# Band rows of values loaded in two transfers per unit, and every store of x on SyncE's queue, in a local and global attention with a mixture of experts

## The chip, the cores and the metric

One core of a Trainium2 chip runs the whole program in one launch. The time is the device time of one execution in microseconds (us); the number for a kernel is the median over its runs. The engines are TensorE (PE in the rows, PEld for its weight loads), VectorE (DVE), ScalarE (ACT), GpSimd (POOL) and SyncE (SP). SP does no arithmetic: it issues transfers (DMAs). ACT and POOL can issue transfers too.

## The reference, cut to what matters

```python
batch, n_heads, seq, head_dim = (8, 8, 576, 64)            # q, k, v
q_d, k_d, v_d = means over 4 neighbouring positions        # 144 positions
out_up = repeat(softmax(q_d k_d^T / 8) v_d, 4)             # global part
mask = abs(pos[:, None] - pos[None, :]) < 4                # local part: a band of 7
out_local = softmax(where(mask, q k^T / 8, -1e9)) v
x = (out_up + out_local)                                   # 4608 tokens x 512
group = argmax(x w_group); expert = argmax(x w_expert[group])
out[token] = weight * relu(x w1[group, expert]) w2[group, expert]
```

There are 4 groups of 4 experts; each token goes to one of 16 experts, with a hidden size of 1024.

## The kernel before, in words

The attention works through 16 units. Unit u takes two batches and two heads (`Attention.unit`), 1152 query rows, and makes 128 of the 512 columns of x for the tokens of its two batches. Per unit the steps are: `load_k`, `load_q`, `load_v` (values pooled for the global part), `load_windows` (band rows of the values for the local part); `s_local`, `s_local_out`, `s_local_exp`, `soft_local` (band scores and their softmax in tile E); `s_down`, `s_down_max`, `s_down_exp`, `out_down`, `turn_down` (global part); `down_store` (L426, L427) writes the small global result to a scratch in DRAM and `load_down` (L431) reads it back into rows 96 to 127 of the tile `vw`; `turn_e` transposes E into `pt`; `x_bank` (L438) multiplies `pt` with `vw` and so makes x, local and global part in one product; `x_bank_out` copies it from PSUM to SBUF; `store_x` (L448) writes the unit's x, 576 KB, to DRAM; `turn_x`, `turn_x_out` and `logits` feed the router. `vw` holds, for 36 blocks of 32 queries, 48 rows of values for each of two heads (rows interleaved), so a row on its way is 64 numbers, 256 bytes.

`load_windows` (L205 to L223) issues four transfers for a unit, one for each head and batch (48 rows x 18 blocks), all from SyncE's queue. The values lie as (batch, head, position, feature). A block's band starts 8 rows ahead of its queries; at the ends of a batch these rows belong to a neighbour in memory, and the mask takes them out. Only the very first and the very last rows of the whole array have no neighbour, so the first and the last unit issue one transfer more (L221, L223). These are 66 transfers in all.

What sets the order of the work is a text, `ORDER`, written out ahead and run step by step (L1389) under a manual schedule: every engine and every queue does its share in exactly this order. A letter at the end of a step names the engine or the queue: A is ScalarE, D VectorE, P GpSimd, S SyncE. `store_x u A` therefore stands in ScalarE's own instruction stream; ScalarE issues the transfer and cannot go past it before it is issued. All loads stand in SyncE's stream. `fill n` is n matmuls that compute nothing that is used. Buffers: K, Q and pooled values have three each, `vw` three (two from unit 14 on), x three (`of`, L102), but from unit 14 on x has one, the one of units 0, 3, ..., 12. Weight tiles of the first expert (`raww`) lie where the attention's input tiles were.

The stretch around the change, in `ORDER` (lines of units 3 to 8):

```
turn_x 4 2; turn_pd_out 7 1 D; store_x 3 A; turn_x_out 4 2 A; load_q 10; turn_x_out 4 0 A; s_down 8; turn_pd_out 7 2 A; fill 12; x_bank 5 0
s_down_max 8; store_x 4 A; s_down_exp 8 0; out_down 7; down_store 6 S; s_down_exp 8 1; load_v 9; x_bank_out 5 2 A; s_local 9 0
```

The four PSUM banks of the pool `ps` are used in turn, so `x_bank 5 0` needs that `turn_x_out 4 0` has emptied one; the three of `psd` likewise, so `s_local 9 0` needs `s_down_exp 8 0`.

At the end of the attention the first expert starts: `early_expert` reads its number, `weights_in` (L826) loads its weights, `turn_in`, `hidden` (L875) and `project` (L921, L923) compute it. Then 14 more experts follow, each with its weights from DRAM, and the leftover rows of the first.

Of the kernel before, what the change touches and what calls it, by code (L numbers as in the profile page):

```python
# [31 lines left out]
NE = 16  # L32
NB = 4
# [20 lines left out]
class Attention:  # L54
# [9 lines left out]
    def __init__(self, tc, q, k, v, idf, xd, left, right, dram):  # L64
        nc = self.nc = tc.nc
        self.tc, self.q, self.k, self.idf = tc, q, k, idf
        n = NTOK * DM
        self.v, self.vm = v[0:n].rearrange("(b h s d) -> b h s d", h=H, s=S, d=D), v[n:].rearrange("(u p f) -> u p f", u=4 * NB, p=SD)
# [15 lines left out]
        one = cp.tile([1, 1], F32, name="one")  # L84
# [1169 lines left out]
turn_x_out 3 2 A; s_local 7 1; load_down 4 S; turn_x_out 3 1 A; turn_pd_out 6 1 D; turn_pd 6 0; logits 3; store_x 1 A; turn_pd 6 2  # L1254
load_v 7; turn_pd_out 6 0 A; s_local_out 7 1; s_local_exp 7 1; soft_local 6; turn_pd_out 6 2 D; x_bank 4 0; down_store 5 S
x_bank 4 2; x_bank_out 4 2 D; scores_out 0; load_windows 5; s_down 7; x_bank 4 1; scores_turn 0; x_bank_out 4 1 A; x_bank_out 4 0 D
scores_turn_out 0; out_down 6; turn_e 6 2; store_x 2 A; out_down_out 6 A; turn_e 6 0; s_down_max 7; turn_down 6; soft_down 6 P
# [9 lines left out]
turn_down_out 7; store_x 5 A; turn_x_out 5 1 A; soft_local 8; turn_x 5 0; load_q 11; x_bank 6 0; x_bank 6 2; s_down 9; pool_k 10 D  # L1267
turn_x_out 5 0 A; turn_pd 8 1; x_bank_out 6 0 A; turn_pd 8 2; x_bank_out 6 2 D; s_local_exp 9 0; s_down_max 9; s_local_exp 9 1
load_windows 7; turn_pd_out 8 1 A; pool_q 10 P; turn_pd_out 8 2 D; down_store 7 S; x_bank 6 1; s_down_exp 9 0; turn_e 8 1; load_k 11
# [3 lines left out]
s_local_out 10 0; soft_down 8 D; out_down_out 8 D; turn_x 6 2; turn_pd_out 9 2 A; s_local_exp 10 0; store_x 6 A; turn_down 8  # L1273
# [12 lines left out]
turn_pd 11 2; turn_e_out 10 1 A; turn_x 8 1; turn_e_out 10 2 A; turn_pd 11 0; turn_pd 11 1; store_x 7 A; turn_pd_out 11 2 A  # L1286
turn_x_out 8 1 A; s_local_out 12 1; soft_down 11 D; load_down 9 S; turn_pd_out 11 0 A; load_k 13; choose 1; store_x 8 A
# [5 lines left out]
turn_pd_out 12 0 A; turn_pd 12 2; soft_local_sum 12 D; store_x 9 A; turn_x 9 0; s_local 13 1; turn_x_out 9 1 A; turn_e_out 11 1 A  # L1293
# [8 lines left out]
turn_pd 13 2; s_local_out 14 1; turn_pd_out 13 0 A; turn_pd_out 13 2 A; store_x 10 A; turn_x 11 2; load_q 15; logits 10; turn_x 11 1  # L1302
# [3 lines left out]
store_x 11 A; s_local_out 15 1; turn_e_out 13 0 A; turn_e_out 13 2 A; s_local 15 0; lists_add 1; s_local_out 15 0; s_local_exp 14 0  # L1306
# [131 lines left out]
```

## Time and profile before

| | us |
|---|---|
| median of 3 runs | 750.79 |
| lowest and highest run | 750.01, 756.18 |
| the profiled execution, its time | 751.14 |
| its span, first to last instruction | 749.4 |

The profile is one execution. It has the busy time of each engine and each group of instructions, what an engine waited for ("<-" and the releaser), and for transfers their issue (a `q` after the engine's name, as SPq) and, where it is known, the time to landing. "PEclk" is the granted clock of TensorE in tenths of full speed (1.00 is 2.4 GHz, 0.50 is 1.2 GHz; numbers between are means over a stretch). The DMA share is the mean busy share of the core's 16 DMA engines. A matmul of fp32 operands stands as two records.

### The profile page before, as it was taken

The numbers are of one execution on the slowest core, as the hardware profiler recorded it, in microseconds if no ns is written. First come the engines' busy times: TensorE is split into PE (matmuls) and PEld (weight loads), VectorE is DVE, ScalarE is ACT, GpSimd is POOL, SyncE is SP. The second block draws the span as 40 slices with busy tenths as digits, with TensorE's granted clock in tenths as the row PEclk, the third lists the DMA queues.
The fourth block names the chain that finished last, engine by engine and source line by source line (L and its number), as shares of the span: only waits on it lengthen the run. The fifth ranks groups of instructions, "written<-read, shape, count | busy, mean of one in ns | idle before, by whom it ended". The sixth has DMA issues, their size and how long they took to land. (4 is left out here: it accounts for less than half of the span.)

```text
span 749.4 us, 20121 instructions
## 1 busy us (share of the span) xinstructions
PE 701.3 (94%) x8212; PEld 639.3 (85%) x8213; DVE 461.6 (62%) x834; ACT 362.7 (48%) x797; POOL 266.2 (36%) x307
## 2 busy tenths in 40 slices
PE   7789978999886979999999999999999999999996
PEld 4577766777665868998999999999999999999985
DVE  7877866999793765654545455464655555565541
ACT  4445535565573426543434444464554554555531
POOL 8975863585543650103111221302213213212211
PEclk9989999999998999999999999999999999999999
DMA  8879999898988463745455545646555665656600
GB/s 297 267 181 282 262 264 243 238 265 229 235 207 235 120 200 117 265 158 196 137 172 170 183 158 176 209 143 211 179 184 186 204 196 193 224 184 211 209 26 25
DMA packets 158243, 146.94 MB, mean 196 GB/s; under 512 B 69396, under 2 KB 129812, under 8 KB 158148
## 3 DMA queue, kind: packets, MB, share of 16 engines
q1 hardware_dynamic: 133540, 115.11, 51.7%
q0 software_dynamic: 7088, 21.66, 8.2%
q10 hardware_dynamic: 17520, 8.85, 4.5%
q8 instruction: 65, 1.06, 0.6%
q14 instruction: 30, 0.25, 0.1%
HBM read 124.29 MB, written 22.29 MB: 196 GB/s over the span
## 5 line engine op out<-in xcount | busy, mean ns | idle before, releaser
L846 POOL DMA_INDIRECT xg<-xd,gi x47 | 48.6, 1035 | 318.7 <-ACT yo L949 289.3
L875 PE MATMUL ph<-xh,w1h 128*128 128x256 f32 (+13 forms) x512 | 161.1, 316 | 0.0
L875 PE MATMUL ph<-xh,w1l 128*128 128x256 f32 (+13 forms) x512 | 156.1, 307 | 0.0
L875 PE MATMUL ph<-xl,w1h 128*128 128x256 f32 (+13 forms) x512 | 156.0, 306 | 0.0
L834 DVE TENSOR_TENSOR w2l<-raww,w2h 128x1024 fp32r<-128x1024 f32 x61 | 74.6, 1224 | 72.0 <-ACT w2h L833 56.5
L923 PE MATMUL y<-hl,w2h 128*128 128x416 f32 (+11 forms) x384 | 115.3, 311 | 0.0
L923 PE MATMUL y<-hh,w2l 128*128 128x416 f32 (+11 forms) x384 | 114.3, 308 | 0.0
L833 ACT ACTIVATE w2h<-raww 128x1024 fp32r<-128x1024 f32 x64 | 67.6, 1057 | 72.3 <-PE y L923 58.2
L875 PEld LDWEIGHTS ph<-xh,w1h 128*128 128x128 f32 x512 | 96.2, 188 | 1.5 <-issue 0.2
L834 DVE TENSOR_TENSOR w1l<-raww,w1h 128x1024 fp32r<-128x1024 f32 x60 | 73.4, 1224 | 38.8 <-ACT w1h L833 31.7
L875 PEld LDWEIGHTS ph<-xl,w1h 128*128 128x128 f32 x512 | 96.3, 188 | 0.9
L875 PEld LDWEIGHTS ph<-xh,w1l 128*128 128x128 f32 x512 | 96.1, 188 | 0.4
L880 DVE SCALAR_TENSOR_TENSOR hl<-ph,hh 128x256 fp32r<-128x256 f32 (+13 forms) x128 | 60.4, 476 | 55.3 <-ACT hh L879 50.6
L879 ACT ACTIVATE hh<-ph 128x256 fp32r<-128x256 f32 (+13 forms) x128 | 53.9, 422 | 75.7 <-PE ph L875 69.6
L923 PE MATMUL y<-hh,w2h 128*128 128x416 f32 (+11 forms) x384 | 87.7, 312 | 0.0
L833 ACT ACTIVATE w1h<-raww 128x1024 fp32r<-128x1024 f32 x64 | 67.5, 1057 | 32.0 <-PE ph L875 19.3
L950 POOL DMA_INDIRECT out_dram<-yo,oi x47 | 48.3, 1028 | 73.1 <-ACT yo L949 37.2
L923 PEld LDWEIGHTS y<-hh,w2l 128*128 128x128 f32 x384 | 72.3, 188 | 0.1
L923 PEld LDWEIGHTS y<-hl,w2h 128*128 128x128 f32 x384 | 72.2, 188 | 0.1
L923 PEld LDWEIGHTS y<-hh,w2h 128*128 128x128 f32 x384 | 62.9, 188 | 0.1
L438 PE MATMUL b_x<-vw,pt 128*32 128x128 f32 x1152 | 41.6, 287 | 6.9 <-DMA vw<-odd 4.3
L855 ACT ACTIVATE xh<-xt 128x256 fp32r<-128x256 f32 (+14 forms) x68 | 27.2, 420 | 34.3 <-PE xt L862 32.2
(225 smaller groups left out, 1287.1 us busy)
## 6 DMA issues: line engine op xcount, KB each, us to landing
raww<-in_moe_w_dram SPq DMA_DIRECT2D x128, 512.0 KB, 4.8
vw<-in_v_dram SPq DMA_DIRECT2D x62, 216.0 KB, 6.9
kt<-in_k_dram SPq DMA_DIRECT2D x16, 582.0 KB, 5.5
qT<-in_q_dram SPq DMA_DIRECT2D x16, 576.0 KB, 6.6
xd<-x ACTq DMA_DIRECT2D x15, 576.0 KB, 6.0
vs<-in_v_dram SPq DMA_DIRECT2D x16, 512.0 KB, 7.4
vw<-odd SPq DMA_DIRECT2D x16, 144.0 KB
odd<-odn SPq DMA_DIRECT2D x16, 128.0 KB
```

The lines of the kernel that those rows point to most:

```text
L438: self.nc.tensor.matmul(pt[32 * j : 32 * j + 32, t], self.of("pt", u)[:, 32 * lin : 32 * lin + 32], self.windows(u)[:, lin], start=True, s ...
L833: self.nc.scalar.activation(hi, raw, AF.Copy)
L834: eng.tensor_tensor(out=lo, in0=raw, in1=hi.bitcast(F32), op=ALU.subtract)
L846: self.nc.gpsimd.indirect_dma_start(out=xg[:w], out_offset=None, in_=self.xd[0:rows], in_offset=bass.IndirectOffsetOnAxis(ap=st["gi"][:w, ...
L855: self.nc.scalar.activation(hi, x, AF.Copy)
L875: nc.tensor.matmul(ph, a[:, k, cs], st[b][:, k], start=(n == 0), stop=(n == 11))
L879: nc.scalar.activation(hh, ph, AF.Relu)
L880: nc.vector.scalar_tensor_tensor(out=hl, in0=ph, scalar=0.0, in1=hh.bitcast(F32), op0=ALU.max, op1=ALU.subtract)
L923: nc.tensor.matmul(y, a[:, f % 2, cs], b, start=(f == 0 and n == 0), stop=(f == 7 and n == 2))
L950: i = nc.gpsimd.indirect_dma_start(out=self.out, out_offset=bass.IndirectOffsetOnAxis(ap=oi, axis=0), in_=yo[:m], in_offset=None, bounds_c ...
```

## The change

On the host the values are put as (pair of batches, head, batch, position, feature), with 8 rows of zeros ahead of the first and behind the last. The two batches of a pair then follow each other for each head, so the 36 blocks of a head have one stride, and `load_windows` issues two transfers of 48 rows x 36 blocks instead of four of 48 x 18; the transfers for the ends go. The rows and bytes are the same. In `ORDER` all `store_x` get the letter S. Most stay where they were; `store_x 5` goes behind `load_windows 7`, `store_x 12` behind `load_windows 14`, `store_x 13` behind `load_windows 15`, and `store_x 14` behind `weights_in 1`. `fill 12` goes. No other step moves.

```diff
-        n = NTOK * DM
-        self.v, self.vm = v[0:n].rearrange("(b h s d) -> b h s d", h=H, s=S, d=D), v[n:].rearrange("(u p f) -> u p f", u=4 * NB, p=SD)
+        n = NTOK * DM + 16 * D
+        self.v, self.vm = v[0:n], v[n:].rearrange("(u p f) -> u p f", u=4 * NB, p=SD)
...
-        s = self.st[u]
-        a = self.v[s["b0"], s["h0"], 0:1, :]
         for h in range(2):
-            dst = self.windows(u)[h : 2 * WW : 2, :, D * h : D * h + D]
-            for b in range(2):
-                o = a.offset + (b * H + h) * S * D
-                lo = 1 if o == 0 else 0
-                hi = NBLK - (o == (B * H - 1) * S * D)
-                dma = lambda rows, l, n: self.nc.sync.dma_start(
-                    out=dst[rows, NBLK * b + l : NBLK * b + l + n],
-                    in_=bass.AP(a.tensor, o + (32 * l - 8 + rows.start) * D, [[D, rows.stop - rows.start], [32 * D, n], [1, D]]),
-                )
-                dma(slice(0, WW), lo, hi - lo)
-                if lo:
-                    dma(slice(8, WW), 0, 1)
-                if hi < NBLK:
-                    dma(slice(0, 40), NBLK - 1, 1)
+            o = self.v.offset + (16 * (u // 4) + 4 * (u % 4) + 2 * h) * S * D
+            self.nc.sync.dma_start(
+                out=self.windows(u)[h : 2 * WW : 2, :, D * h : D * h + D],
+                in_=bass.AP(self.v.tensor, o, [[D, WW], [32 * D, 2 * NBLK], [1, D]]),
+            )
...
-turn_x 4 2; turn_pd_out 7 1 D; store_x 3 A; turn_x_out 4 2 A; load_q 10; turn_x_out 4 0 A; s_down 8; turn_pd_out 7 2 A; fill 12; x_bank 5 0
+turn_x 4 2; turn_pd_out 7 1 D; store_x 3 S; turn_x_out 4 2 A; load_q 10; turn_x_out 4 0 A; s_down 8; turn_pd_out 7 2 A; x_bank 5 0
...
-s_down_max 8; store_x 4 A; s_down_exp 8 0; out_down 7; down_store 6 S; s_down_exp 8 1; load_v 9; x_bank_out 5 2 A; s_local 9 0
+s_down_max 8; store_x 4 S; s_down_exp 8 0; out_down 7; down_store 6 S; s_down_exp 8 1; load_v 9; x_bank_out 5 2 A; s_local 9 0
...
-turn_e 15 0; store_x 14 A; turn_e_out 15 0 D; turn_x_out 14 0 D; turn_x 14 2; turn_x 14 1; turn_x_out 14 1 D; turn_x_out 14 2 A
+turn_e 15 0; turn_e_out 15 0 D; turn_x_out 14 0 D; turn_x 14 2; turn_x 14 1; turn_x_out 14 1 D; turn_x_out 14 2 A
...
-weights_split 0 w2 P; weights_in 1; turn_e 15 2; turn_e_out 15 2 D; x_bank 15 0; turn_in 2; x_bank_out 15 0 A; x_bank 15 1
+weights_split 0 w2 P; weights_in 1; store_x 14 S; turn_e 15 2; turn_e_out 15 2 D; x_bank 15 0; turn_in 2; x_bank_out 15 0 A; x_bank 15 1
...
-            a = _np.concatenate([a.reshape(-1), _np.concatenate([x.reshape(4 * NB, -1) for x in (two, one)], axis=1).reshape(-1)])
+            a = _np.pad(a.reshape(NB, 2, H, S, D).transpose(0, 2, 1, 3, 4).reshape(-1), (8 * D, 8 * D))
+            a = _np.concatenate([a, _np.concatenate([x.reshape(4 * NB, -1) for x in (two, one)], axis=1).reshape(-1)])
```

## Rows read from the trace of the kernel before

**Rows 1.** The page: the span in 40 equal slices of 18.7 us, tenths of TensorE's granted clock and of the DMA engines' busy share.

```profile
PEclk9989999999998999999999999999999999999999
DMA  8879999898988463745455545646555665656600
```

**Rows 2.** Busy time by stretch of the attention: start:end, length, then busy us (and instructions) of PE, PEld, DVE, ACT, POOL, the granted clock, the DMA share and GB/s.

```profile
58.00:110.00 52.00, 45.34 (x1122) 36.05 (x1121) 39.69 (x93) 26.01 (x89) 34.29 (x40) 0.98 0.99 278
110.00:126.00 16.00, 13.27 (x310) 10.81 (x313) 7.63 (x19) 7.51 (x23) 5.61 (x7) 0.84 0.94 215
126.00:176.00 50.00, 45.92 (x1119) 36.50 (x1112) 45.08 (x101) 31.11 (x105) 33.04 (x35) 1.00 0.95 250
176.00:216.00 40.00, 35.87 (x857) 27.58 (x855) 34.02 (x88) 24.41 (x80) 25.37 (x44) 1.00 0.92 233
216.00:230.00 14.00, 9.11 (x128) 6.57 (x130) 10.39 (x32) 7.07 (x21) 3.85 (x5) 0.92 0.73 171
```

**Rows 3.** ScalarE in order of time, 97 to 118 us: start, length, engine, line, operation, what it writes and reads, count, and in brackets the idle time ahead of it with what ended it. `xd<-x` is store_x (units 2, 3 and 4 here), `Pd` is s_down_exp, `xT` is turn_x_out.

```profile
97.70 0.42 ACTq L448 DMA_DIRECT2D xd<-x  x1
...
103.10 0.41 ACT L173 ACTIVATE PdT<-b_pd 128x288 f32<-128x288 f32 x1
110.70 0.37 ACTq L448 DMA_DIRECT2D xd<-x  x1
111.12 0.87 ACT L173 ACTIVATE xT<-b_xt 128x384 f32<-128x384 f32 x2 [7.61 <-DMA xd<-x]
...
113.17 0.55 ACT L288 ACTIVATE E<-E 128x342 f32<-128x342 f32 x1
117.17 0.39 ACTq L448 DMA_DIRECT2D xd<-x  x1
117.61 0.38 ACT L345 ACTIVATE Pd<-b_d,mg 128x144 f32<-128x144 f32 x1 [3.89 <-DVE od L175]
```

**Rows 4.** TensorE in order of time, 104 to 126 us. L311 is s_down 8, L158 the fill, the first L438 x_bank 5, L265 s_local 9, the last L438 x_bank 6.

```profile
104.17 1.17 PE L311 MATMUL b_d<-kd,qd 64*128 64x144 f32 x20
...
107.79 4.13 PE L158 MATMUL lg<-idf 128*128 128x128 f32 x21 [1.93 <-issue]
111.85 2.17 PE L438 MATMUL b_x<-vw,pt 128*32 128x128 f32 x72
...
118.50 1.36 PE L265 MATMUL b_s<-kt,qT 64*32 64x38 f32 x72 [2.61 <-ACT Pd L345]
...
125.21 1.52 PE L438 MATMUL b_x<-vw,pt 128*32 128x128 f32 x48
```

**Rows 5.** VectorE in order of time: the wait ahead of x_bank_out 4, the last instruction of s_down_max 8 (L336), and its next one.

```profile
95.99 1.02 DVE L175 COPY x<-b_x 128x384 f32<-128x384 f32 x2 [3.34 <-DMA xd<-x]
...
108.51 0.50 DVE L336 TENSOR_SCALAR mg<-mg 128x5 f32<-128x5 f32 x1
113.75 0.87 DVE L296 TENSOR_REDUCE sl<-E 128x18 f32<-128x684 f32 x1 [4.74 <-ACT E L288]
```

**Rows 6.** SyncE's queue in order of time, issues merged by line: start, time from the first issue's start to the last one's end, count. L215 is load_windows (units 5, 6, then 15), L431 load_down (units 5, 6, then 14).

```profile
88.12 7.22 SPq L215 DMA_DIRECT2D vw<-in_v_dram  x4
95.46 0.70 SPq L431 DMA_DIRECT2D vw<-odd  x1
...
103.71 7.08 SPq L215 DMA_DIRECT2D vw<-in_v_dram  x4
110.83 0.71 SPq L431 DMA_DIRECT2D vw<-odd  x1
...
218.41 6.33 SPq L215 DMA_DIRECT2D vw<-in_v_dram  x5
226.05 0.75 SPq L431 DMA_DIRECT2D vw<-odd  x1
```

**Rows 7.** Issue times of the two kinds of transfer that the change touches, from the views of lines L215 and L448: engine, operation, count, ns of one issue (least, median, most), first and last start. Then their sizes with the median us from issue to landing.

```profile
L215 SPq DMA_DIRECT2D vw<-in_v_dram x66: 576/672/3110, 13.0 to 222.0; - x66
L448 ACTq DMA_DIRECT2D xd<-x x15: 366/367/418, 48.4 to 234.4; - x15
...
vw<-in_v_dram SPq DMA_DIRECT2D x62, 216.0 KB, 6.9
xd<-x ACTq DMA_DIRECT2D x15, 576.0 KB, 6.0
xd<-x SPq DMA_DIRECT2D x1, 576.0 KB, 7.0
odd<-odn SPq DMA_DIRECT2D x16, 16.0 KB, 2.2
```

**Rows 8.** SyncE's own waits up to 260 us: line, what released it, us in total, times, longest.

```profile
SPq L215 <- DMA vs<-in_v_dram: 5.0, 3, 3.3
SPq L215 <- DMA kt<-in_k_dram: 3.3, 2, 2.0
```

**Rows 9.** The end of the attention in order of time, 229 to 244 us: x_bank 14 on TensorE, store_x 14 on ScalarE's queue, x_bank_out 15, turn_x 15.

```profile
229.78 4.07 PE L438 MATMUL b_x<-vw,pt 128*32 128x128 f32 x72 [4.32 <-DMA vw<-odd]
...
234.43 0.37 ACTq L448 DMA_DIRECT2D xd<-x  x1
...
242.62 0.87 ACT L173 ACTIVATE x<-b_x 128x384 f32<-128x384 f32 x2 [3.07 <-DMA xd<-x]
...
243.54 1.20 PE L453 MATMUL b_xt<-idf,x 128*128 128x128 f32 x9 [1.44 <-ACT x L173]
```

More of the change, by code (lines that the diff above doesn't have):

```diff
@@ L1266 @@
 turn_e_out 7 1 A; pool_k 9 P; s_local_out 9 0; turn_e_out 7 2 A; turn_x 5 1; turn_x 5 2; turn_x_out 5 2 A; s_local_out 9 1
-turn_down_out 7; store_x 5 A; turn_x_out 5 1 A; soft_local 8; turn_x 5 0; load_q 11; x_bank 6 0; x_bank 6 2; s_down 9; pool_k 10 D
+turn_down_out 7; turn_x_out 5 1 A; soft_local 8; turn_x 5 0; load_q 11; x_bank 6 0; x_bank 6 2; s_down 9; pool_k 10 D
 turn_x_out 5 0 A; turn_pd 8 1; x_bank_out 6 0 A; turn_pd 8 2; x_bank_out 6 2 D; s_local_exp 9 0; s_down_max 9; s_local_exp 9 1
-load_windows 7; turn_pd_out 8 1 A; pool_q 10 P; turn_pd_out 8 2 D; down_store 7 S; x_bank 6 1; s_down_exp 9 0; turn_e 8 1; load_k 11
+load_windows 7; store_x 5 S; turn_pd_out 8 1 A; pool_q 10 P; turn_pd_out 8 2 D; down_store 7 S; x_bank 6 1; s_down_exp 9 0; turn_e 8 1; load_k 11
 soft_local_sum 9 P; x_bank_out 6 1 A; turn_pd 8 0; load_k 12; turn_e 8 2; turn_pd_out 8 0 A; s_local 10 0; turn_e_out 8 1 A
@@ L1285 @@
 s_down_exp 11 2; turn_e 10 2; soft_down 10 D; s_local 12 1; turn_down_out 10; pool_v 11; load_windows 9; s_local_out 12 0; load_v 12
-turn_pd 11 2; turn_e_out 10 1 A; turn_x 8 1; turn_e_out 10 2 A; turn_pd 11 0; turn_pd 11 1; store_x 7 A; turn_pd_out 11 2 A
-turn_x_out 8 1 A; s_local_out 12 1; soft_down 11 D; load_down 9 S; turn_pd_out 11 0 A; load_k 13; choose 1; store_x 8 A
+turn_pd 11 2; turn_e_out 10 1 A; turn_x 8 1; turn_e_out 10 2 A; turn_pd 11 0; turn_pd 11 1; store_x 7 S; turn_pd_out 11 2 A
+turn_x_out 8 1 A; s_local_out 12 1; soft_down 11 D; load_down 9 S; turn_pd_out 11 0 A; load_k 13; choose 1; store_x 8 S
 s_local_exp 12 0; lists_add 0; lists_out 0; soft_local_sum 11 D; x_bank 9 0; down_store 10 S; turn_pd_out 11 1 A; x_bank 9 1
@@ L1301 @@
 x_bank_out 11 1 A; soft_local 13; load_windows 12; turn_pd 13 1; pool_v 13; turn_pd 13 0; turn_pd_out 13 1 A; down_store 12 S
-turn_pd 13 2; s_local_out 14 1; turn_pd_out 13 0 A; turn_pd_out 13 2 A; store_x 10 A; turn_x 11 2; load_q 15; logits 10; turn_x 11 1
+turn_pd 13 2; s_local_out 14 1; turn_pd_out 13 0 A; turn_pd_out 13 2 A; store_x 10 S; turn_x 11 2; load_q 15; logits 10; turn_x 11 1
 turn_x_out 11 2 A; lists_places 1; turn_x 11 0; turn_x_out 11 1 A; s_local 14 0; turn_x_out 11 0 A; out_down 13; load_v 14
@@ L1310 @@
 count 2; turn_x_out 12 0 A; turn_pd 14 0; turn_pd 14 2; turn_x_out 12 1 A; turn_pd_out 14 0 A; turn_pd_out 14 2 A; pool_k 15 P
-pick_early; turn_pd 14 1; s_down 15; load_v 15; turn_pd_out 14 1 A; turn_x 12 2; store_x 12 A; turn_x_out 12 2 A; load_windows 14
+pick_early; turn_pd 14 1; s_down 15; load_v 15; turn_pd_out 14 1 A; turn_x 12 2; turn_x_out 12 2 A; load_windows 14; store_x 12 S
 soft_down 14 P; out_down 14; x_bank 13 1; s_down_max 15; weight 2; s_down_exp 15 2; out_down_out 14 A; turn_down 14; x_bank 13 2
 s_down_exp 15 0; s_down_exp 15 1; x_bank_out 13 1 A; pool_v 15; x_bank 13 0; turn_pd 15 0; x_bank_out 13 2 A; turn_down_out 14
-soft_local 14; x_bank_out 13 0 A; turn_pd_out 15 0 A; places_out 2; store_x 13 A; turn_pd 15 1; down_store 14 S; turn_x 13 2
-turn_pd 15 2; turn_pd_out 15 1 A; logits 12; turn_pd_out 15 2 D; load_windows 15; s_local_exp 15 1; turn_x_out 13 2 A; out_down 15
+soft_local 14; x_bank_out 13 0 A; turn_pd_out 15 0 A; places_out 2; turn_pd 15 1; down_store 14 S; turn_x 13 2
+turn_pd 15 2; turn_pd_out 15 1 A; logits 12; turn_pd_out 15 2 D; load_windows 15; store_x 13 S; s_local_exp 15 1; turn_x_out 13 2 A; out_down 15
 lists_places 2; turn_x 13 0; soft_down 15 P; turn_x 13 1; lists 2 P; out_down_out 15 A; turn_down 15; turn_x_out 13 1 A
```

10 lines of the change are left out of this document (5 added, 5 removed).

## The prediction

> **What bounds the kernel now.** I read the page's slices first [rows 1], then the busy times by stretch [rows 2], then single engines in order of time where a stretch stood out. The slices split the run at about 245 us: up to there (the attention) the DMA engines are busy 0.8 to 0.9 of the time, behind it (the experts) about half, with TensorE at full clock. The change touches only the attention, and the experts follow its end step by step, so what the end of the attention gains or loses, the total gains or loses.
>
> In the attention two things are near full at once. From 58 to 110 us the DMA engines are busy 0.99 of the time; from 110 to 216 us it is 0.92 to 0.95, with TensorE at 0.90 to 0.92 of its time (45.92 of 50, 35.87 of 40) and VectorE close behind [rows 2]. One stretch falls out: 110 to 126 us has TensorE at 13.27 of 16, VectorE at 7.63, and a granted clock of 0.84, between the two levels. What it waits for is ScalarE. ScalarE's last copy ahead of store_x 3 ends at 103.51; store_x 3 is issued only at 110.70, and the next copy starts at 111.12 after 7.61 us of idling, released by a landing of `xd<-x`, so of an earlier store [rows 3]. The tile of unit 3 was long ready: the store waits for another store to be finished, and ScalarE's stream stands behind it. Window loads are released in the same way by landings of tiles that they have nothing to do with [rows 8], so I read this as a limit on transfers under way: each new one waits until an older one has landed. store_x 4 does it again: ScalarE's previous instruction ends at 113.72, the store goes out at 117.17, and s_down_exp 8 starts behind it at 117.61 [rows 3]. (The row names a VectorE copy as releaser; that one stands later in the order and can't be what s_down_exp needs.)
>
> TensorE ends s_down 8 at 105.34, passes the time with the fill, idles 1.93 us, and starts x_bank 5 at 111.85; later it idles 2.61 us until s_local 9 starts at 118.50 [rows 4]. VectorE idles 4.74 us ahead of its instruction at 113.75 [rows 5].
>
> The second place is the end. load_windows 15 takes SyncE from 218.41 to 224.74, load_down 14 goes out at 226.05 [rows 6], and TensorE idles 4.32 us until x_bank 14 at 229.78. Then x_bank_out 15 waits for the landing of store_x 14, since both use one buffer: store at 234.43, copy at 242.62 [rows 9].
>
> **The change part by part.**
> *ScalarE loses 15 issues.* At 0.367 us each that is 5.5 us of its queue [rows 7], but ScalarE is idle half of the time [rows 2]; by itself I cost it at nothing, 0 to 1 us gained. What counts is the two waits. Without them the copies that x_bank 5 needs run from 103.5 us, and x_bank 5 can follow s_down 8 at 105.3: 111.85 - 105.3 = 6.5 us earlier. s_down_exp 8 then waits for VectorE's maximum, ready at 109.01 [rows 5]; two activations of 0.38 and two read-outs end by 110.0 [rows 3], so s_local 9 moves from 118.50 to about 110.0: 8.5 us. That is the upper end. `fill 12` is part of these 6.5 us and isn't counted again.
>
> *What is late next: the loads.* x_bank 6, at 125.21 [rows 4], needs load_down 6, issued at 110.83 [rows 6]. No view gives that transfer's landing; with the 6.9 us of a window load [rows 7] it lands at 117.7, so x_bank 6 gains at most 7.5 us if the loads stay where they were. They don't quite: store_x 4, which left at 117.17, now stands in front of windows 6 in the same queue, and 576 KB at 215 to 278 GB/s [rows 2] take 2.1 to 2.7 us. That leaves about 5. From 126 to 216 us the DMA engines are idle 0.05 x 50 + 0.08 x 40 = 5.7 us in all, so loads can just keep up with a shift of this size, not with one much larger. I take 4.5 us; ends 0 (the loads give all of it back) and 8.5.
>
> *SyncE: 34 issues fewer, 15 more.* 34 x 0.672 - 15 x 0.367 = 22.8 - 5.5 = 17.3 us less issuing, if an issue of twice the blocks costs the same; if it costs twice, the windows save nothing and SyncE has 5.5 us more. Neither is seen before, since no transfer of 36 blocks and 48 rows is there. A large part of the 7.22 and 7.08 us that four window issues take [rows 6] is no issuing at all (4 x 0.672 = 2.7): the last issue of a unit takes up to 3.1 us [rows 7], it waits for the queue to drain, and the data to drain are the same. So I take 0 for the stretches where the DMA engines are full, -1.5 to +1.5.
>
> *The end.* load_windows 15 now has two issues (1.3 us at least), then store_x 13 (0.37), then load_down 14. By issue alone it could go out up to 6.33 - 1.34 - 0.37 = 4.6 us earlier. But its data follow 864 KB of windows and 576 KB of x in one queue: from 218.41, some 2.2 us to the start (the quickest landing, [rows 7]) and 1440 KB at 215 to 278 GB/s, 5.2 to 6.7 us, end at 225.8 to 227.3, so x_bank 14 could start near 227.5 instead of 229.78. I take 1.5 us, between 0 (the last issue still drains for 2.7 us and load_down 14 leaves at 226) and 2.5. store_x 14 moves behind four weight transfers, but x of unit 14 isn't ready before they are issued, so I let the shift pass to x_bank_out 15 and to all experts.
>
> Here a page speaks against the change. The landing of store_x 14 took at least until x_bank_out 15 at 242.62, 8.2 us from ScalarE's queue beside weights on SyncE's [rows 9], while store_x 15, from SyncE's queue, landed in 7.0 [rows 7]. The Trainium skill, "DMA: Bandwidth & Descriptors", section "Queues, rings and completion order", says that a DMA engine takes turns between the queues that have work for it, so a store on a queue of its own gets every second turn, and one moved to the loads' queue waits behind all of them. By that rule the end would gain nothing and the sum below would be 1.5 us less; the 8.2 against 7.0 us show no such advantage here.
>
> *Other edits.* The zero rows replace neighbours' rows that the mask took out; the order of values on the host is no device time; the three transfers of one block at the ends go with the 34. Nothing for these. VectorE's 3.34 us ahead of x_bank_out 4 [rows 5], a wait for store_x 1 to land, may shrink as that store no longer waits for ScalarE; it lies before the DMA-bound point, so I take 0, up to 2.5.
>
> **Sum.** 4.5 + 1.5 = 6.0 us. The profiled execution took 751.14 us (span 749.4), so 745.1; the median of the runs shown is 0.35 lower, and I say 745.0. A measurement of this kernel can tell about 1% (7.5 us) from no change, so this counts as the same.
>
> **Rivals.**
> *The loads give it back.* For it: the DMA share of 0.92 to 0.99 from 58 to 216 us [rows 2], and the same packets as before. Against: 5.7 us of idle DMA time, and the wait that goes is ScalarE's, not a load's. Then only the end gains, 0 to 2.5 us: 748.6 to 751, say 749.5.
>
> *More of it stays.* If shorter issuing on SyncE lets loads start earlier, the 8.5 us hold and the end adds 2.5: 751.14 - 11.0 = 740.1. For it: 17.3 us less issuing. Against: the drain of the queue.
>
> *SyncE inherits the wait (slower).* A store on SyncE that waits for an older transfer holds up every load behind it, where it held up copies before. If store_x 3 stood 7.6 us on SyncE, load_q 10, load_v 8, load_k 10, windows 6 and load_down 6 would all start that much later. It decides when the wait exceeds the lead that the loads have, about the 6.9 us that a window load needs to land: then the DMA engines run dry for up to 7.6 us, of which the idle 2.5 us of 126 to 176 us can be made up, and the end comes 5 us later: 756. Against: with 34 transfers fewer, an older transfer lies further back in time.
>
> *The change doesn't do what it says:* an issue of 36 blocks takes 1.34 us. Then SyncE gains nothing at the windows, and the time lies between the forecast and the first rival, 747.
>
> **How the numbers follow.** Forecast with its own range 743.3 to 748.5 (this last rival in it): 0.45. Loads give it back, 748.5 to 752: 0.20. More stays, 737.5 to 743.3: 0.27. Slower, 752 to 760: 0.08, half of it past 1%. The range 739.0 to 751.5 leaves out about 0.07 below (a quarter of the third case) and 0.11 above. Faster by over 1% (under 743.3) is the third case, 0.29 with the edge of the first; slower by over 1% (over 758.3) 0.04; the rest, 0.67, is within 1%.
>
> **What would show it.** ScalarE's row at 111.12 without the 7.61 us, and no idle time of that kind ahead of s_down_exp 8; TensorE's x_bank 5 directly behind s_down 8; the stretch that answers to 110 to 126 us at a clock near 1.00; x_bank 6 at about 120 us; x_bank 14 some 6 us earlier than 229.78. L215 with 32 issues of about 0.67 us would bear out the issue cost, 1.3 us the last rival. It is wrong if x_bank 6 stays near 125 (loads), if SyncE shows a store waiting 5 us or more, or if TensorE's idle time returns behind `vw` landings between 126 and 216 us.

## The result, and the profile after

The changed kernel took 757.19 us (median of 20 runs, 749.97 to 769.32), the kernel before 752.0 us beside it (20 runs, 748.48 to 760.02). The ratio is 1.0057, with a 95% interval of 1.0031 to 1.0083: 0.57% slower, 4.3 us, where 6 us faster was forecast. A second measurement on another occasion gave 1.0052 (1.0010 to 1.0093). The profiled execution has a span of 755.3 us against 749.4. All ratios here leave out runs that a disturbance of the chip lengthened, so a ratio can be nearer to 1 than its median looks (mid_only below).

The page's slices after, as in [rows 1]:

```profile
PEclk9998999989998999999999999999999999999999
DMA  8879799997879444765364645656555566666600
```

Busy time by stretch, columns as in [rows 2]:

```profile
58.00:110.00 52.00, 45.47 (x1082) 35.20 (x1081) 35.53 (x83) 26.19 (x89) 27.74 (x32) 0.93 0.93 256
110.00:126.00 16.00, 13.81 (x344) 10.61 (x346) 13.63 (x30) 7.74 (x24) 12.95 (x15) 0.97 1.08 262
126.00:176.00 50.00, 44.13 (x1010) 35.25 (x1003) 41.83 (x92) 28.94 (x98) 31.86 (x33) 0.93 0.96 244
176.00:216.00 40.00, 34.90 (x885) 27.87 (x882) 32.14 (x81) 23.17 (x71) 22.73 (x42) 0.96 0.91 225
216.00:230.00 14.00, 13.88 (x186) 10.04 (x185) 11.58 (x39) 9.11 (x30) 4.76 (x5) 0.88 0.72 163
```

The stretch from 110 to 126 us did what the forecast said: granted clock 0.97 for 0.84, VectorE 13.63 for 7.63. The stretches around it lost: the clock is 0.93 from 58 to 110 and from 126 to 176 us, where it was 0.98 and 1.00. These levels belong to the one execution: in a second profile of the changed kernel (after_again below) the clock is 0.97, 0.89 and 1.00 from 58, 110 and 126 us on.

ScalarE after, the copies that stood behind store_x 3 and s_down_exp 8 behind store_x 4 (line numbers are 11 lower than before from L226 on), against [rows 3]:

```profile
109.24 0.40 ACT L173 ACTIVATE PdT<-b_pd 128x288 f32<-128x288 f32 x1
111.30 0.87 ACT L173 ACTIVATE xT<-b_xt 128x384 f32<-128x384 f32 x2 [1.66 <-PE b_xt L442]
...
115.64 0.38 ACT L334 ACTIVATE Pd<-b_d,mg 128x144 f32<-128x144 f32 x1 [0.99 <-DVE mg L325]
```

The waits of 7.61 and 3.89 us are 1.66 and 0.99, and they end on TensorE and VectorE, not on a transfer. TensorE after, against [rows 4] (s_down 8, x_bank 5, s_local 9 in two parts, x_bank 6):

```profile
111.19 1.17 PE L300 MATMUL b_d<-kd,qd 64*128 64x144 f32 x20
112.29 2.69 PE L427 MATMUL b_x<-vw,pt 128*32 128x128 f32 x72
...
116.77 0.47 PE L254 MATMUL b_s<-kt,qT 64*32 64x38 f32 x31
118.74 0.58 PE L254 MATMUL b_s<-kt,qT 64*32 64x38 f32 x41 [1.50 <-issue]
...
124.78 1.52 PE L427 MATMUL b_x<-vw,pt 128*32 128x128 f32 x48 [0.31 <-ACT xT L173]
```

x_bank 5 follows s_down 8 directly, as forecast. But s_down 8 starts at 111.19, 7.0 us later than before, so x_bank 5 at 112.29 is no earlier than it was (111.85), and x_bank 6 at 124.78 is where it was (125.21).

SyncE at the end of the attention, against [rows 6, 9] (L437 is store_x 12, 13 and 14, L209 windows 15, L420 load_down 14 and 15, L815 the first weights), and the line of all window issues against [rows 7] (shortest, median, longest in ns):

```profile
213.14 3.62 SPq L437 DMA_DIRECT2D xd<-x  x1
...
224.22 1.53 SPq L209 DMA_DIRECT2D vw<-in_v_dram  x2
225.84 1.90 SPq L437 DMA_DIRECT2D xd<-x  x1
228.71 0.75 SPq L420 DMA_DIRECT2D vw<-odd  x1
...
232.38 1.00 SPq L815 DMA_DIRECT2D raww<-in_moe_w_dram  x2
233.49 1.26 SPq L420 DMA_DIRECT2D vw<-odd  x1
234.97 1.81 SPq L815 DMA_DIRECT2D raww<-in_moe_w_dram  x2
237.22 0.37 SPq L437 DMA_DIRECT2D xd<-x  x1
```

```profile
L209 SPq DMA_DIRECT2D vw<-in_v_dram x32: 582/1088/4206, 13.0 to 224.9; - x32
```

One thing ahead of the prediction was told too broadly: store_x 0 kept its place on ScalarE's queue, so 14 stores changed queues, not all of them (and not the 15 of the prediction); store_x 15 was on SyncE's already.

**Where the two executions part.** I matched ScalarE's instructions one to one and read how much later each one starts after than before: +4.2 us at 97 us, -2.0 at 117.6 (the wait that went), -0.4 at 128, +3.2 at 170, +5.6 at 220, +1.7 at 235 (load_down 14 came sooner), +6.3 at 246 (the first expert), +5.5 at the end. So there are three questions: what became of the 6 us gained at 111 to 118, what was lost between 128 and 220, and what was lost between 235 and 246.

### The profile page after: what moved, and what is told of

It reads as the page before. It is cut to its first block, busy times and chain, and to the rows that moved or that the text cites. A ratio compares the mean times of both kernels' runs of the same rounds, so it can differ in the third digit from the quotient of the medians.

```text
span 755.3 us, 20037 instructions
## 1 busy us (share of the span) xinstructions
PE 704.9 (93%) x8189; PEld 639.8 (85%) x8189; DVE 462.0 (61%) x834; ACT 363.0 (48%) x797; POOL 267.2 (35%) x307
```

## The experiments

Ratios are to the kernel before, run beside each kernel on the same chip; each kernel has 12 runs, the two with half windows 4.

| kernel | what differs from before | ratio (95%) |
|---|---|---|
| windows_only | two window transfers | 0.9990 (0.9959 to 1.0022) |
| stores_only | all the stores' moves, no fill | 1.0058 (1.0023 to 1.0092) |
| tail_back | after, store_x 13 and 14 as before | 1.0018 (0.9982 to 1.0053) |
| two_stores | store_x 3 and 4 on S, no fill | 0.9984 (0.9952 to 1.0016) |
| old_place | after, store_x 13 on S ahead of windows 15 | 1.0034 (0.9992 to 1.0076) |
| down_first | load_down 14 ahead of windows 15 | 1.0002 (0.9969 to 1.0036) |
| no_fill | fill 12 gone | 1.0010 (0.9973 to 1.0046) |
| two_fill | store_x 3 and 4 on S | 0.9981 (0.9938 to 1.0023) |
| tail_fill | tail_back with the fill | 1.0024 (0.9987 to 1.0061) |
| after_again | the whole change | 1.0052 (1.0010 to 1.0093) |
| tail_13 | store_x 13 on S behind windows 15 | 1.0011 (0.9976 to 1.0046) |
| mid_only | stores 1, 2, 5 to 12 on S | 1.0008 (0.9957 to 1.0060), median 757.32 |
| best_mix | two window transfers, store_x 3 and 4 on S | 0.9964 (0.9924 to 1.0003) |
| best_again | the same once more | 1.0012 (0.9977 to 1.0048) |

**The two halves.** windows_only has the diff's host part and load_windows, with the old ORDER; stores_only the new ORDER with the old load_windows.

> The kernel before with the change of the values alone: pairs of batches, zero rows, two window transfers a unit. All stores, and the fill, stay as before. In the trace after, TensorE has idle times that no semaphore ends (about 15 us in all between 50 and 210 us, about 8 us before), each ending some 1.0 to 1.3 us behind the end of a 16 KB packet of the queue that carries TensorE's instructions. Theory F (fetch): the larger window transfers put more in front of these packets, so the stalls belong to the windows: they stand here too, 12 to 16 us of them, ScalarE's 7.61 us stays, and the time is 3 to 6 us over before. Theory S (stores): the loss comes from the stores in SyncE's queue, so this kernel is within 1.5 us of before and its stalls sum to 7 to 10 us. Theory T (tail): the loss is the first expert's late gather behind store_x 13, so here too the time is within 1.5 us of before.

> The kernel before with the new places and queues of the stores and without fill 12; windows in four transfers from the old layout. Theory F: ScalarE's 7.61 us go, the stalls without a semaphore stay at 7 to 10 us, and the time is 3 to 6 us under before. Theory S: the loads are late behind stores, the time is 3 to 6 us over before, as in the kernel after (757.2 against 752.0). Theory T: ScalarE's wait goes (8 us early at 120 us), the first expert's gather starts late, and the time is within 3 us of before.

The windows cost nothing and bring nothing that can be told (0.9990); the new ORDER, all the stores' moves with the fill gone, carries the whole loss (1.0058, the same as the change). Theory F (TensorE's own instructions arrive late) falls as the cause of the loss: it asked for 3 to 6 us over before in windows_only, and stores_only, with the old window transfers, has 13 us of idle times without a semaphore between 50 and 210 us for 8 in before. Theory S (the stores make the loads late) and theory T (the tail: the first expert's gather is late) are left.

**Parts of the stores.**

```diff
 tail_back (on after)
-load_windows 15; store_x 13 S; ...        weights_in 1; store_x 14 S;
+places_out 2; store_x 13 A; turn_pd 15 1  turn_e 15 0; store_x 14 A;
 two_stores (on before)
-store_x 3 A; ... fill 12; x_bank 5 0      store_x 4 A;
+store_x 3 S; ... x_bank 5 0               store_x 4 S;
```

> The kernel after with store_x 13 and store_x 14 back on ScalarE's queue at the places they had before. Theory T: the gather then starts as store_x 13 lands early, the shift of 3.5 to 5 us between 236 and 246 us goes, and the time is 3.5 to 5 us under after (752.5 to 753.5). Theories F and S: the first expert starts when x of unit 15 is there anyway, so the time stays within 1.5 us of after; S would allow 1 to 2 us less as two of the fourteen moved stores leave the queue.

> The kernel before with only store_x 3 and store_x 4 moved to SyncE's queue, and without fill 12: the two stores at which ScalarE stood 7.61 and 3.89 us. Windows in four transfers, the other stores as before. My forecast's step says that taking these two waits away brings 4.5 us (0 to 8.5). Theory F expects 746 to 748, since the stalls stay as before. Theory S expects little, 750 to 753, if loads behind the two stores are late in turn. Theory T expects the gain whole, 744 to 748, as the end is that of before.

tail_back, 2.9 us under the change by the ratios, lies between what theory T asks (3.5 to 5) and no gain; the two intervals overlap. two_stores is what my forecast should have been right on, and it brought 1.2 us (from 3.6 gained to 1.2 lost), not 4.5. On ScalarE the gain is there: relative to before it stands at +3.9 us at 100 us and -3.4 at 117.6. At 128 it is +1.2 again.

**Half windows and the step at the end.**

```diff
 half_before (on before), half_two (on two_stores)
-dma(slice(0, WW), lo, hi - lo)
+dma(slice(0, WW // 2), lo, hi - lo)
 down_first (on before)
-logits 12; turn_pd_out 15 2 D; load_windows 15; ...  load_down 14 S; down_store 15 S
+logits 12; turn_pd_out 15 2 D; ...  load_down 14 S; load_windows 15; down_store 15 S
 old_place (on after)
-places_out 2; turn_pd 15 1; ...  load_windows 15; store_x 13 S;
+places_out 2; store_x 13 S; turn_pd 15 1; ...  load_windows 15;
```

> The kernel before with window transfers of the first 24 of a band's 48 rows (216 KB a unit less, the other rows are left as they were, so the local part of x is not complete). It is the base for the next kernel. All theories: with 16 x 432 KB less to load, the DMA engines are no longer full between 58 and 110 us. Theory L (loads set the pace) expects the attention to end 5 us or more earlier than before; theory F (TensorE's own instructions arrive late because the transfers stand in front of them) expects the idle times without a semaphore to shrink from 8 us to 4 or less, and 2 to 5 us from that; neither expects ScalarE's wait for store_x 3 to be over 3 us.

> The kernel two_stores (store_x 3 and 4 on SyncE's queue, no fill 12) with the same half windows. With whole windows it gained 7 us on ScalarE up to 118 us and had given it back by 126 us, with TensorE idle for no semaphore and at the lower clock in between, while load_down 6 had landed 6 us before x_bank 6 needed it. Theory F: with fewer transfers in front of its instructions TensorE does not stall between 104 and 126 us (under 1 us in all), and what is gained there against half_before stays until 128 us. Theory L: the same, since loads have room. Theory C (clock): without the fill TensorE falls to the lower clock anyway, the stretch 104 to 126 us stays near 0.8, and nothing is gained against half_before.

Their whole times (1178.03 and 1176.09 us) can't be compared with the others: with the local part of x incomplete, tokens go to other experts. Up to 230 us the traces can be read. half_before ends the attention only 0.8 us earlier than before (at 220 us), not 5: theory L falls as the bound of the whole attention. half_two gains nothing on half_before: from 100 to 128 us half_before wins 4.5 us against before, half_two 1.1. Theory F fails too: half_before still has 7 us of idle times for no semaphore, where 4 or less were asked, and half_two idles 1.5 and 1.8 us at 114 and 106 us. Its clock, 0.62 and 0.52 from 120 to 128 us, is what theory C expected.

> The kernel before with one step moved: load_down 14 goes ahead of load_windows 15 in SyncE's queue. x_bank 14 waits 4.32 us for load_down 14, which stands behind the 864 KB of windows 15, not needed before x_bank 15, 15 us later. If the forecast's step on the end is right (the queue ahead of load_down 14 is what x_bank 14 waits for), load_down 14 goes out at 219 to 221, TensorE's 4.32 us shrink to under 1, and the time is 3 to 4 us under before. The rival: x_bank 15, the gather and the weights behind windows 15 set the end of the attention, then windows 15 is late, and the time stays within 1 us of before or rises.

> The kernel after with store_x 13 still on SyncE's queue, but at the place it had before: ahead of load_windows 15 and not behind it. Between 232 and 238 us the first expert's gather starts about 1.2 us behind the landing of store_x 13 in the kernel after (232.22, gather 233.37), in stores_only, and in the kernel before (224.83, gather 226.14). Theory T1 (the place): the store holds the tiles on which the expert's tiles lie, so going first it lands some 3 us earlier, the gather starts at 227 to 230, and the time is 2.5 to 4 us under after (753 to 754.5). Theory T2 (the queue): a store on SyncE's queue lands late wherever it stands, behind the loads issued before it; then the gather stays at 231 to 234 and the time within 1.5 us of after. Theory T3 (it is store_x 14, not 13): no change either.

In down_first load_down 14 went out at 222.37 for 226.05, x_bank 14 no longer waits on it, and ScalarE's copies behind it are 2.1 to 3.1 us earlier than before at 232 to 235 us. At 246 us they are 3.4 later: TensorE waits 2.74 us for the gather and 2.93 for load_down 15. So an earlier x_bank 14 does not by itself bring the end forward. old_place lands between the theories (1.0034); its gather says more, below.

**The fill, and the whole change again.** no_fill takes only `fill 12; ` out of before, two_fill puts it back into two_stores, tail_fill into tail_back.

> The kernel before without fill 12, nothing else changed; store_x 3 and 4 still hold ScalarE. In the kernels without the fill so far TensorE's granted clock fell to 0.50 for 4 to 9 us on real work between 112 and 126 us (tail_back 116 to 124 us, two_stores 120 to 124, stores_only 0.57 at 120 to 124); in the kernel before the low stretch (0.57 at 108 to 112 us) lies on the fill. Theory C (the fill takes the low clock on itself): without it x_bank 5 and what follows run at 0.50, s_down 9 starts 2 to 4 us later than 126.66, and the time is 1 to 3 us over before. Theory N (the fill only passes time): the same start of s_down 9 within 1 us and the time within 1 us of before.

> The kernel two_stores (store_x 3 and 4 on SyncE's queue) with fill 12 kept: taking away ScalarE's two waits alone. Theory C: the fill takes some 2 us at full clock, or 4 at the low one, behind s_down 8, but the work behind it runs at full clock, s_down 9 starts at 122 to 124.5 (before 126.66, two_stores 127.85), and the time is 2 to 4 us under before. Theory N: the fill is plain cost, the time is that of two_stores plus 1 to 2 us, so 0 to 1 us over before. Theory P (TensorE's own work, its stalls for instructions and its clock set the pace over tens of us, and a wait that goes is only used up by another): within 1.5 us of before, whatever the clock does.

> The kernel after with store_x 13 and 14 back on ScalarE at their old places, and with fill 12: the two parts of the change that theories T and C hold for harmful are undone. If both are right it is the best kernel: 3 us under tail_back, 1 to 3 us under before. Theory T alone: as tail_back, 0 to 2 us over before. Theory S (stores in SyncE's queue make the loss): 1 to 3 us over before, as tail_back or worse.

> The kernel after once more, on the same chip as the three others and with a second profile. The ratio to before should come out at 1.003 to 1.008 again. Its second profile tells what in the first was of this program and what of the one execution: theory F expects TensorE's idle times without a semaphore at the same instructions (x_bank 1, logits 0, s_local 8 and 9, the s_local at 163.73), within 1 us of each length; if they stand elsewhere, they belong to the moment. Theory T expects the gather within 1.5 us behind store_x 13's landing again and the first expert 4 us late.

The fill makes no difference that can be told in any of the three pairs (1.0010 without it; 0.9981 with it against 0.9984; 1.0024 against 1.0018; each interval reaches some 3 us to either side), though in the two profiles below the clock moves as theory C says. TensorE's stretch from 112 to 124 us, first in tail_back, then in two_fill (columns as in [rows 2]):

```profile
112.00:116.00 4.00, 2.23 (x88) 1.66 (x84) 3.36 (x10) 1.06 (x5) 3.60 (x5) 0.88 0.98 181
116.00:120.00 4.00, 4.00 (x92) 3.29 (x84) 1.49 (x3) 1.35 (x3) 1.29 (x2) 0.50 0.95 274
120.00:124.00 4.00, 4.00 (x31) 2.52 (x33) 3.42 (x6) 1.11 (x3) 3.36 (x5) 0.50 1.12 272
```

```profile
112.00:116.00 4.00, 4.00 (x101) 3.34 (x99) 1.65 (x2) 2.65 (x12) 3.68 (x5) 1.00 1.08 248
116.00:120.00 4.00, 3.07 (x136) 2.28 (x134) 3.24 (x12) 1.53 (x6) 0.02 (x1) 1.00 0.76 153
120.00:124.00 4.00, 3.64 (x76) 2.61 (x79) 3.86 (x7) 1.68 (x5) 2.96 (x4) 1.00 1.06 280
```

In tail_back TensorE was busy 2.23 of 4 us and then ran 8 us at 1.2 GHz, on real work. In two_fill the clock stays full, the gain lasts until 137 us, and there x_bank 7 stands 2.31 us until its load_down has landed (137.40; the row has no releaser):

```profile
137.49 1.21 PE L438 MATMUL b_x<-vw,pt 128*32 128x128 f32 x24 [2.31 <-issue]
```

Two ways to lose the same gain. Theory P fits: two_fill is 1.4 us faster, within its 1.5; the interval (4.7 faster to 1.7 slower) does not rule out the 2 us that theory C asks.

after_again repeats the ratio (1.0052) and the late gather, 1.15 us behind the landing of store_x 13. Of TensorE's idle times without a semaphore six stand at the same instructions as in after, but not with the lengths that theory F asks for: 4.55 us is 1.25.

**The shares of the stores, and the parts put together.**

```diff
 tail_13 (on before): store_x 13 A out of its place; load_windows 15; store_x 13 S
 mid_only (on before): store_x 1, 2, 6 to 11 A -> S; store_x 5 and 12 S behind load_windows 7 and 14
 best_mix, best_again (on windows_only): store_x 3 and 4 A -> S
```

> The kernel before with one store moved: store_x 13 on SyncE's queue behind load_windows 15, as in the kernel after; everything else as before. So far the way from ScalarE's copy at 235.36 us to the first expert's copy at 246.21 us (times of the kernel before) grew by 4.6 and 4.8 us in the two profiles of after and 7.3 in stores_only, by 2.7 in old_place, and by 0 to 1.7 us where store_x 13 stayed on ScalarE. Theory T (store_x 13 alone does it): that way grows by 4 to 7 us here too, the gather starts within 1.5 us behind the store's landing, and the time is 2 to 5 us over before. Rivals: it takes store_x 14 behind the weights as well, or the stores of the middle; then the way grows by under 2 us and the time stays within 1 us of before.

> The kernel before with the stores of units 1, 2 and 5 to 12 on SyncE's queue at the places of the kernel after; store_x 3, 4, 13 and 14 and the fill as before, windows in four transfers. Theory S (a store in the loads' queue makes the loads behind it late, which TensorE waits for at an x_bank): 1 to 3 us over before, which with the tail's part is the whole loss of after. Theory T alone (the loss is the tail's): within 1 us of before. A gain of over 1 us would say that the stores of the middle belong there.

> Two window transfers with the new layout, store_x 3 and 4 on SyncE's queue, the fill and all else as before: the parts of the change that no run so far holds for harmful, put together. My forecast's sum (the two waits 4.5 us, the end 1.5 us) would make it 6 us under before; from the runs, two_fill (ratio 0.9981) and windows_only (0.999), I expect 1 to 4 us under before. If the loads take back what ScalarE gains, as x_bank 7 and 8 starting 0.1 to 0.2 us behind the landing of their load_down say, it is within 1.5 us of before.

> The kernel best_mix once more (two window transfers, store_x 3 and 4 on SyncE's queue, all else as before), on another occasion, since its interval (0.9924 to 1.0003) touches one. If the two waits and the window issues bring what is left of the forecast, the ratio is 0.994 to 0.998 again and the two measurements together lie below one; if the loads or the gather take it back, it is 0.998 to 1.002. In the profile the first gather starts about 1.1 us behind the end of the list of its rows, or, where that is later, 1.1 us behind the landing of store_x 13, as in every run so far.

mid_only tells nothing from no change (1.0008, the widest interval of all). best_mix looked like a gain and best_again took it back; no version here beats the kernel before. In tail_13 the way of which its text speaks, ScalarE's from 235.36 to 246.21 us, grew by 5.1 us and the gather started 1.10 us behind the store's landing, as theory T says; the time is not 2 to 5 us over before but 0.8. That way grew by 6.5 us in down_first too, with store_x 13 at its old place, so it does not tell a late gather from an early x_bank 14; below I take a longer one. tail_13 is still the most useful run, for two reasons.

*First: up to 217 us it is the kernel before, instruction for instruction, and so is down_first. So their profiles are further executions of the stretch that my forecast rests on.* ScalarE at store_x 3, first in tail_13, then in down_first:

```profile
106.01 0.37 ACTq L448 DMA_DIRECT2D xd<-x  x1
107.23 0.87 ACT L173 ACTIVATE xT<-b_xt 128x384 f32<-128x384 f32 x2 [0.77 <-PE b_xt L453]
```

```profile
110.79 0.37 ACTq L448 DMA_DIRECT2D xd<-x  x1
111.20 0.87 ACT L173 ACTIVATE xT<-b_xt 128x384 f32<-128x384 f32 x2 [8.64 <-DMA xd<-x]
```

And TensorE's x_bank 6, with what went wrong ahead of it in tail_13; then in down_first:

```profile
107.12 1.17 PE L311 MATMUL b_d<-kd,qd 64*128 64x144 f32 x20
108.22 2.94 PE L158 MATMUL lg<-idf 128*128 128x128 f32 x24
111.10 2.17 PE L438 MATMUL b_x<-vw,pt 128*32 128x128 f32 x72
...
121.10 0.40 PE L265 MATMUL b_s<-kt,qT 64*32 64x38 f32 x20 [2.17 <-issue]
...
122.80 2.18 PE L453 MATMUL b_xt<-idf,x 128*128 128x128 f32 x9
124.98 1.74 PE L438 MATMUL b_x<-vw,pt 128*32 128x128 f32 x48
```

```profile
125.39 1.52 PE L438 MATMUL b_x<-vw,pt 128*32 128x128 f32 x48 [0.21 <-ACT xT L173]
```

ScalarE's wait was 7.61 us in the execution of [rows 3], 8.64 in down_first and 0.77 in tail_13, with the same program. x_bank 6 starts at 125.21, 125.39 and 124.98. The wait lasts until store_x 2 has landed, which took 13.0 us from its issue in before (97.70 to 110.68), 14.0 in down_first and 5.3 in tail_13. Its length is not what it costs: in tail_13, where it is absent, ScalarE is already 3.0 us later than in before at 97 us (0.9 earlier in down_first), and TensorE comes to s_down 8 three us later. From there to x_bank 6 it is 3.2 us quicker, though it idles for no semaphore at 121.10 and turns x at the lower clock (2.18 us for nine records; 1.51 in before). The executions that come early wait, the one that comes late does not, and x_bank 6 starts at the same time.

*Second: the tail.* The expert's tiles (`xg` of the gather and the raw weights) lie in the room of the input pool, in which x of unit 13 stands. The gather reads only rows of the first three pairs of batches (`NTOK * 3 // 4` in the kernel), so it does not need what store_x 13 writes; it needs the room. SyncE's waits say so for the weights; from 218 to 236 us in after, then in tail_13:

```profile
SPq L815 <- DMA xd<-x: 1.7, 1, 1.7
```

```profile
SPq L826 <- DMA xd<-x: 1.3, 1, 1.3
```

The columns are the waiting line, what it waited for, us in total, times, longest. The same row stands in after_again (2.0) and stores_only (1.4); before and tail_back have none. The gather and the list of its rows, before and after:

```profile
224.90 0.17 DVE L760 TENSOR_SCALAR gi<-rv 128x4 int32<-128x4 f32 x1
...
226.14 1.29 POOL L846 DMA_INDIRECT xg<-xd,gi  x1 [5.38 <-DMA vw<-in_v_dram]
```

```profile
230.47 0.17 DVE L749 TENSOR_SCALAR gi<-rv 128x4 int32<-128x4 f32 x1
...
233.37 1.29 POOL L835 DMA_INDIRECT xg<-xd,gi  x1 [7.03 <-DVE E L291]
```

In us, with the landing of store_x 13 as the trace has it:

| kernel | list done | store_x 13 landed | gather |
|---|---|---|---|
| before | 225.07 | 224.83 | 226.14 |
| tail_back | 228.77 | 228.14 | 229.84 |
| two_fill | 228.64 | 228.47 | 229.71 |
| old_place | 229.37 | 227.02 | 230.44 |
| after | 230.64 | 232.22 | 233.37 |
| after_again | 230.86 | 232.71 | 233.86 |
| stores_only | 227.54 | 229.35 | 230.44 |
| tail_13 | 223.50 | 225.34 | 226.44 |

The gather starts 1.07 to 1.15 us behind the later of the two, in all eight and in the ten profiles that are not in the table. With store_x 13 behind windows 15 that is the store, 1.6 to 1.9 us late; in old_place, on the same queue but ahead of windows 15, it is the list again. So the place does it, not the queue. (In best_mix, on ScalarE's queue at its old place, the store is the later one too, but by 0.4 us.) (The page names for the row of after a VectorE instruction that is no source of the gather; the row of SyncE and the table tell the store.) TensorE's first two `turn_in` then wait for the two transfers of the gather; in tail_13:

```profile
232.22 0.30 PE L862 MATMUL xt<-idf,xg 128*128 128x128 f32 x1 [1.29 <-issue]
235.16 0.47 PE L862 MATMUL xt<-idf,xg 128*128 128x128 f32 x1 [2.63 <-DMA xg<-xd,gi]
```

The row at 232.22 names no releaser, but it starts 0.09 us behind the landing of the first one (232.13). Together that is 3.9 us in tail_13, 3.2 in after, 3.9 in after_again and 5.7 in stores_only; in before it is nothing. The wait is not theirs alone: in nine others (named in the next paragraph) it is 0 to 3.2 us, 1.7 in the mean. There the gather is on time by its list, x_bank 14 is early, and the gather is the next to be late.

What this is worth: between ScalarE's instructions at 220.15 and 246.21 us of before, the four profiles with the store behind windows 15 lose 0.6 to 2.8 us against before, 1.5 in the mean; nine others (without windows_only, whose profile is of its longest run, down_first, which moves windows 15, and the halves) gain 1.1 in the mean (from 3.3 gained to 1.4 lost). The difference is 2.6 us, 0.34%, as large as that of the two means of TensorE's wait (4.2 and 1.7 us). The times agree in size: the four measurements with the store there (after, after_again, stores_only, tail_13) have a mean ratio of 1.0045, the other eleven of the table 1.0002, though these differ in other parts too. For tail_13 alone the time does not show it: 1.0011 reaches from 1.8 us faster to 3.5 us slower. So the late gather is shown, and its price is an estimate.

## Why the prediction was wrong

*What bounds the kernel.* The reading of ScalarE's wait as a limit on transfers under way was right as to what held it: the trace has one of eight completion semaphores on each transfer of SyncE and ScalarE, in turn, and each waits for the landing of the one eight before (store_x 3 has that of store_x 2, which landed at 110.68, and goes out at 110.70). Wrong was to take from it that the wait sets the pace there.

*The term of ScalarE's waits, 4.5 us ("ends 0 and 8.5"), is the step that failed.* What it said of the waits came true: 7.61 to 1.66, 3.89 to 0.99, x_bank 5 behind s_down 8, clock 0.97. What it said of the times did not: x_bank 5 was to come 6.5 us earlier and came 0.4 later. Nor did the price: two_fill, which takes away these two waits and nothing else, is 1.4 us faster, from 4.7 faster to 1.7 slower. The wait was priced from one execution, and another execution of the same program has 0.77 us in its place and reaches x_bank 6 at the same time. The low end, 0, was in the range; the choice of 4.5 between the ends was the error.

*What is late next.* The forecast named the loads, at x_bank 6: load_down 6 was to land at 117.7. It did, in before (117.71), with some luck: the 16 load_down of before took 3.1 to 7.4 us. But in after it landed at 121.80 and x_bank 6 started at 124.78, held by a copy; it was not the load. Loads do pace single steps: x_bank 8 starts 0.1 to 0.2 us behind its load_down in before (151.0) and after (150.2), x_bank 7 in two_fill. Between them I read TensorE itself as the limit, by its stalls and its clock; no run isolates that. The rival "the loads give it back" was right in its sum for this term and only in part in its reason.

*SyncE's issuing at 0.* Right for the time: windows_only is 0.9990. An issue of 36 blocks takes 0.58 us at its shortest, and 12 of the 32 stay under 0.65, as short as an issue of 18 blocks [rows 7], so the last rival (1.34 us) is out. The sum was wrong: 15 stores took SyncE 18.2 us in after, not 15 x 0.367 = 5.5, and its issues of windows and stores together went from 76.1 us to 67.1, 9.0 us less and not 17.3. That the long issues (up to 4.2 us) wait for the queue to drain, as the prediction says, no run shows.

*The end, 1.5 us.* By the wait ahead of it x_bank 14 came 2.8 us sooner, more than the 1.5 of the forecast: 4.32 us [rows 9] became 1.51. (By the clock it is later, 232.56 for 229.78, since everything is 5.6 us late at 220 us.) The sentence that failed is "I let the shift pass to x_bank_out 15 and to all experts". Behind x_bank 14 comes the first expert, which waits for its gather and its weights; they wait for the tiles under them, so for store_x 13, which the change put behind 864 KB of windows. down_first shows both halves: x_bank 14 earlier, the expert not. In place of 1.5 us gained, the four profiles above show 1.5 lost. TensorE at 230 to 242 us in after (x_bank 14, then the first expert's turn_in):

```profile
232.56 2.71 PE L427 MATMUL b_x<-vw,pt 128*32 128x128 f32 x72 [1.51 <-DMA vw<-odd]
...
240.00 0.30 PE L851 MATMUL xt<-idf,xg 128*128 128x128 f32 x1 [1.87 <-issue]
241.64 0.47 PE L851 MATMUL xt<-idf,xg 128*128 128x128 f32 x1 [1.34 <-DMA xg<-xd,gi]
```

*The rule of turns.* The Trainium skill, "DMA: Bandwidth & Descriptors", section "Queues, rings and completion order", says that a DMA engine takes turns between the queues that have work for it; by that, the prediction said, the moved store loses its turns and the end gains nothing. The end gained nothing, but not so: store_x 13 took 6.0 us from issue to landing on ScalarE's queue (218.84 to 224.83) and 6.4 behind the windows on SyncE's (225.84 to 232.22); over all profiles it is 4.2 to 6.6 us on ScalarE's queue and 4.5 to 6.6 on SyncE's. What cost was the later start: it left 7.0 us later than before, where the list of rows was 5.6 us later.

*The rival on the other side* (SyncE inherits the wait, 756 us) has the time nearly right and the mechanism not, which is luck: SyncE does stand in the issue of a store, 3.6 us at the longest in after (213.14) and not 7.6, and load_down 6 still landed 3.0 us ahead of x_bank 6.

*What is open.* Of some 4.1 us (the mean of 1.0057 and 1.0052) the tail accounts for about 2.6 by the estimate above; no run of a single change shows that much in its time. The other 1.5 are what tail_back and tail_fill still show (1.0018, 1.0024), and both intervals hold 1. The stores of the middle may be it; mid_only is too wide to say. Open too is what was lost between 128 and 220 us, 6.0 us in after: two_stores, two_fill and mid_only lose 4.1, 5.8 and 5.8 there, and their ratios are 0.9984, 0.9981 and 1.0008.

## What to carry to other kernels

Before a wait is priced, look at it in a second execution of the same program: a wait of 7.6 us that is 0.8 us in the next, with the same time behind it, is not worth its length. When a store is moved, ask what lies next in the room of its tile: the loads and gathers that take it over wait for the landing, so a store that is the last reader of a buffer belongs ahead of bulk loads that are not urgent, whichever queue it is on. And follow an early step at least to the next point where two chains meet before its gain is passed on to the end.

## What the runs showed of the hardware

TensorE idles at places where no semaphore holds it. In the profiles of after and after_again this is at the same instruction (the 64th of 72 of an s_local), with a different length:

```profile
163.73 0.35 PE L254 MATMUL b_s<-kt,qT 64*32 64x38 f32 x9 [4.55 <-issue]
```

```profile
164.33 0.28 PE L254 MATMUL b_s<-kt,qT 64*32 64x38 f32 x9 [1.25 <-issue]
```

Its own instructions come as transfers of 16 KB over the DMA engines, 65 of them in the run:

```profile
q8 instruction: 65, 1.06, 0.6%
```

TensorE has 16,567 records in before (matmuls, weight loads and its sequencer's own), 255 for each of the 65 packets. Numbered in order of time, the records that end an idle time of 0.7 us or more without a semaphore (50 to 215 us, all 18 profiles) stand 192 to 194 behind a multiple of 256 in 133 of 134 cases; the other is the wait for load_down 7 in two_fill, shown above. Waits of that length that end on a semaphore are spread over the remainders. And in the single packets of the traces of before and after, each such idle time ends 1.2 to 1.6 us behind the end of a packet (for 163.73 a packet from 161.2 to 162.4). So TensorE is late there for the next part of its own program, by 0.7 to 4.6 us a time. That the full DMA engines make the packets late is my reading; no run here takes the fetch away. The lengths change from one execution to the next, and with the clock that falls behind them (tail_back) they may be one source of the spread of a per cent and more over the runs of one kernel. They do not set the time alone: the profile with the most of them, 17.5 us in tail_back, is of the shortest of these executions (747.4 us).
